# Start of a conditioned attention and MLP block: order of the first loads, modulation, low parts, and the fourth pair's loads

## The chip, the core and the metric

The kernel runs on one core of a Trainium2 chip. The time is that of one execution on the device, in microseconds (us); the median of three runs of the kernel before is shown below, with one further run under the profiler. The engines are TensorE (PE; its weight loads are shown as PEld), VectorE (DVE), ScalarE (ACT), GpSimd (POOL) and SyncE (SP), which issues nearly all transfers.

## The reference

The input x has 2048 tokens of 512 values, c is one row of 512. All is float32.

```
mod = silu(c) @ w_mod                  # six rows of 512: sa, ca, ga, sb, cb, gb
h = layernorm(x) * (1 + ca) + sa
q, k, v = split(h @ wqkv)              # 32 heads of 16
x = x + ga * (softmax(q k^T / 4) v @ wo)
h = layernorm(x) * (1 + cb) + sb
out = x + gb * (mish(h @ w1 + b1) @ w2)   # 1792 in the middle
```

## The kernel before

Each float32 factor of a projection is held as a high part that is rounded to TensorE's fp32r format and a low part, the rest (names in `_h`, `h` and `_l`, `l`: `h_h` and `h_l`, `wh` and `wl`, `qh` and `ql`). A product is three matmuls: high times high, high times low, low times high. `hi_copy(eng, ...)` makes a high part on the engine that is given ("a" ACT, "p" POOL, "v" DVE), `lo_sub` a low part.

Every engine's order is that of the code: the kernel is written under a manual schedule. A small planner (`pe_queue`, `pe_run`, `unit`, hooks at numbered steps) hands out PE's matmuls among the other work; `free_banks` decides from the names of what a piece reads and writes which pieces depend on one another.

The program has four parts.

1. The start (to about 50 us), which holds nearly all of the change. SP loads c (as `cc`, 128 x 4), the two modulation weights that come first (`wma`, sa and ca, 1 MB each), tokens (`xt`, tiles of 128 tokens) and slices of wqkv (`wr`). `first_norm` takes the statistics of tokens 0 to 511 on DVE (BN_STATS, BN_AGGR) and the scales on POOL; `first_apply` normalises a tile; `sil` is silu(c); `modc` has the modulation as columns, `modc[:, 0]` sa and `modc[:, 1]` 1 + ca. Both come from eight 32x512 matmuls (one for each 128 rows of the weight, in 32 partitions each), a copy to `row`, and sixteen matmuls with the 0/1 column `sel`, which add the four parts and turn the row into a column. Then a loop over blocks of 512 tokens (`tb` = 0 to 3): `tr_tb` transposes the normalised tiles on PE into PSUM, makes `h_h` on ACT, the full value `hf` on DVE and `h_l` = `hf` − `h_h` on DVE for the quarters k in `LOV[tb]`, else on POOL; `qk_unit` and `v_unit` project; `stats_tb` and `apply_tb` normalise the blocks that follow. `slice_split` makes `wh` and `wl` of a slice of wqkv.
2. The maxima (to about 102 us): the first two head pairs' scores are made once and DVE takes the maxima of their rows (L555). They are put into the query tiles by four loads from `mt` to `qa` (L577). Projections fill PE.
3. The main loop of steps t: for each pair of heads scores (L588), exponentials on ACT (L591), values (L606), and the scores and maxima of a pair to come (L539, L541). `load_pair(pp)` loads queries (`qa`, L313) and keys (`ka`, L322) of a pair from scratch memory at a hook; the step of the hook counts in half steps of t, negative before the main loop.
4. The tail of the MLP.

`qa` and `ka` hold constant rows (zeros, ones) which are set once at the start; `zer` is a tile of zeros. POOL sets all of them before it does anything else.

Of the kernel before, what the change touches and what calls it, by code (L numbers as in the profile page):

```python
# [18 lines left out]
def adaln_block(ctx: ExitStack, tc: tile.TileContext, x, wqkv, wo, w1, b1, w2, c, w_mod, out):  # L19
    nc = tc.nc  # L20
    P = 128
# [27 lines left out]
    out = out[0]  # L49

    ctx.enter_context(tc.manual_schedule())
    nc.scalar.preload_act_table_set("natural_log_exp_and_others")
# [19 lines left out]
    nc.gpsimd.memset(hcap, HCAP)  # L72
    ones = cst.tile([P, 1], F32, name="ones")
    nc.gpsimd.memset(ones, 1.0)
    sel = cst.tile([P, 1], F32, name="sel")
    nc.gpsimd.memset(sel, 0.0)
    for k in range(DK):
        nc.gpsimd.memset(sel[32 * k:32 * k + 1, :], 1.0)
    lows = cst.tile([P, 1], F32, name="lows")
    nc.vector.tensor_reduce(out=lows[:32], in_=ident[:32, :32].rearrange("p (a v q) -> p v a q", a=4, v=2)[:, 1], op=ALU.add,  # L80
                            axis=AX.XY)
# [18 lines left out]
    def lo_sub(eng, lo, src, hi):  # L100
        (nc.gpsimd if eng == "p" else nc.vector).tensor_sub(lo, src, hi.bitcast(F32))  # L101
# [66 lines left out]
    def free_banks():  # L168


        seen = []
        for i in nc.cur_bb.bb.instructions:
            banks, names, made = set(), set(), set()
            for a in (*i.outs, *i.ins):
                v = getattr(a, "bass_ap", None)
                if v is not None and v.tensor.name != ring_t.tensor.name:
                    names.add(v.tensor.name)
                    if any(a is w for w in i.outs):
                        made.add(v.tensor.name)
# [148 lines left out]

    with ExitStack() as es:
        lp = es.enter_context(tc.tile_pool(name="lp", bufs=1))  # L330
        cc = lp.tile([P, DK], F32, name="cc")
        nc.sync.dma_start(cc, c.rearrange("o (k p) -> p (o k)", p=P))
        xts = []

        def load_x(t):
            xt = lp.tile([P, D], F32, tag="xt", name="xt", bufs=16)
            nc.sync.dma_start(xt, x[t * P:(t + 1) * P, :])
            xts.append(xt)

        wma = [lp.tile([P, DK, D], F32, name=f"wma{i}") for i in range(2)]  # L340
        for i in range(2):
            nc.sync.dma_start(wma[i], w_mod[:, i * D:(i + 1) * D].rearrange("(k p) m -> p k m", p=P))
        for t in range(4):
            load_x(t)
        slice_load(1, 0, lp, lp)
        slice_load(0, 0, lp, lp)
        for t in range(4, 8):
            load_x(t)
# [2 lines left out]
            load_x(t)  # L351
        slice_load(0, 1, pw)
        zer = lp.tile([P, TB], F32, name="zer")
        nc.gpsimd.memset(zer, 0.0)
        for i in range(NR):
            nc.gpsimd.memset(qa[i].bitcast(F32), 0.0)
        for i in range(2):
            nc.gpsimd.memset(ka[i].bitcast(F32), 1.0)

        e = lp.tile([P, DK], F32, name="sil_e")  # L360
        nc.scalar.activation(e, cc, AF.Exp, scale=-1.0)
        nc.vector.tensor_scalar_add(e, e, 1.0)
        nc.vector.reciprocal(e, e)
        nc.vector.tensor_mul(sil, cc, e)

        rss = {}

# [19 lines left out]
        def first_norm():  # L387

            mv = lp.tile([P, 4, 2], F32, tag="ln_mv4", name="ln_mv4", bufs=2)
            rs = lp.tile([P, 4, 4], F32, tag="ln_rs4", name="ln_rs4", bufs=3)  # L390
            for h in range(2):
                two = slice(2 * h, 2 * h + 2)
                for i in range(2 * h, 2 * h + 2):
                    st_ = lp.tile([P, 6], F32, tag="ln_st", name="ln_st", bufs=4)
                    nc.vector.bn_stats(out=st_, in_=xts[i])
                    nc.vector.bn_aggr(out=mv[:, i, :], in_=st_)
                nc.gpsimd.tensor_scalar(rs[:, 0, two], mv[:, two, 1], 1.0, EPS, op0=ALU.mult, op1=ALU.add)
                nc.gpsimd.tensor_scalar(rs[:, 3, two], mv[:, two, 0], -1.0, 0.0, op0=ALU.mult, op1=ALU.add)
                nc.gpsimd.tensor_tensor(rs[:, 1, two], rs[:, 0, two], nhalf.to_broadcast([P, 2]), op=ALU.pow)
                nc.gpsimd.tensor_mul(rs[:, 2, two], rs[:, 3, two], rs[:, 1, two])  # L400
                if h == 0:
                    hi_k = split_hi(1, 0)
            return rs, hi_k

        def split_hi(kind, i, eng="p"):
# [4 lines left out]
        def split_lo(kind, i, hi):  # L410
            lo = lp.tile([P, DK, P], F32R, tag="wl", name="wl", bufs=2)
            lo_sub("p", lo, slices[kind, i], hi)
            slices[kind, i] = (hi, lo)

        def first_apply(rs, i, eng):
            xt = xts[i]
            if eng == "a":
                nc.scalar.activation(xt, xt, AF.Identity, scale=rs[:, 1, i:i + 1], bias=rs[:, 2, i:i + 1])
            else:
                nc.vector.tensor_scalar(xt, xt, rs[:, 1, i:i + 1], rs[:, 2, i:i + 1], op0=ALU.mult, op1=ALU.add)  # L420

        def first_tr():
            pts = [bank(("ring", "ms", "ring", "acc")[k]) for k in range(DK)]
            for ii in ((0,), (1,), (2, 3)):
                for k in range(DK):
                    for i in ii:
                        nc.tensor.transpose(pts[k][:, i * P:(i + 1) * P], xts[i][:, k * P:(k + 1) * P], ident)
            return pts

        def tr_tb(tb, ks=range(DK), pts=None):  # L430
            for k in ks:
                if pts is None:
                    pt = bank(("ring", "ms", "ring", "acc")[k])
                    for i in range(4):
                        nc.tensor.transpose(pt[:, i * P:(i + 1) * P], xts[4 * tb + i][:, k * P:(k + 1) * P], ident)
# [4 lines left out]
                nc.scalar.activation(h_h[:, k, s], pt, AF.Identity, scale=modc[:, 1, k:k + 1], bias=modc[:, 0, k:k + 1])  # L440
                nc.vector.tensor_scalar(hf, pt, modc[:, 1, k:k + 1], modc[:, 0, k:k + 1], op0=ALU.mult, op1=ALU.add)
                lo_sub("v" if k in LOV[tb] else "p", h_l[:, k, s], hf, h_h[:, k, s])

        rs, hi_k = first_norm()
        pr, pm = [], bank()[:, :2 * DK].rearrange("p (i k) -> p i k", k=DK)
        for i in range(2):
            pr.append(ring())
            for k in range(DK):
                nc.tensor.matmul(pr[i][32 * k:32 * k + 32, :], sil[:, k:k + 1].to_broadcast([P, 32]), wma[i][:, k, :],
                                 start=True, stop=True)  # L450
        for i in range(2):
            row = lp.tile([P, D], F32, tag="hf", name="row", bufs=6)
            nc.scalar.copy(row, pr[i])
            for k in range(DK):
                nc.tensor.matmul(pm[:, i, k:k + 1], row[:, k * P:(k + 1) * P], sel, start=True, stop=True)
        for i in range(2):
            first_apply(rs, i, "a")
        split_lo(1, 0, hi_k)
        hi_q = split_hi(0, 0, "a")
        split_lo(0, 0, hi_q)  # L460
        first_apply(rs, 2, "a")
        first_apply(rs, 3, "v")
        nc.vector.tensor_scalar_add(modc[:, 1, :], pm[:, 1, :], 1.0)
        nc.vector.tensor_copy(modc[:, 0, :], pm[:, 0, :])
        stats_tb(1)
        tr_tb(0, pts=first_tr())
        apply_tb(1)
# [11 lines left out]
        for tb in range(NB):  # L479
            if tb + 2 < NB:  # L480
                stats_tb(tb + 2)
            if tb == 0:
                slice_split(2, 0, eng="v")
            parts = []
            early = []
            for kind in (1, 0) if tb == 0 else (1,):
# [1063 lines left out]
```

## Time and profile before

| what | value |
| --- | --- |
| median of 3 runs | 1690.82 us (1689.89 to 1692.33) |
| profiled execution | 1691.02 us, of it 1689.2 us span |
| PE busy | 1667.3 us, 99% of the span |
| DVE, ACT, POOL busy | 1441.5, 1355.1, 821.1 us |
| chain that ended last | PE 91%, DVE 3%, ACT 3%, DMA 2%, POOL 1% |

The busy share is a mean over the span. The start differs from the rest: PE begins at 9.21 us. In the timeline, each row has the start, the length, the engine, the line of the kernel, the operation, and what is written and read; a bracket at its end tells how long the engine had stood idle before and whose work released it. In rows of groups, the numbers behind the first bar are the busy time in us and the mean of one in ns.

### The profile page before, as it was taken

What the parts mean: (1) busy time and instruction counts of PE and PEld (TensorE: products, weight loads), DVE (VectorE), ACT (ScalarE), POOL (GpSimd) and SP (SyncE); (2) the same over time, 40 slices, a digit from 0 to 9 for tenths busy, and PEclk for the clock granted to TensorE, in tenths of its full rate; (3) what the DMA queues carried; (4) which work ended last, traced back from release to release, by engine and by line L of the source; (5) the groups of instructions that cost most, each with busy time, mean ns of one, the idle gap of its engine ahead of it and who ended that gap; (6) DMA issues with size and microseconds to landing.
All of it is one profiled execution on the core that took longest, in us unless ns stands there. A gap on an engine that the chain in (4) does not pass through costs nothing.

```text
span 1689.2 us, 33772 instructions
## 1 busy us (share of the span) xinstructions
PE 1667.3 (99%) x12418; PEld 921.5 (55%) x12418; DVE 1441.5 (85%) x2369; ACT 1355.1 (80%) x2612; POOL 821.1 (49%) x843
## 2 busy tenths in 40 slices
PE   7999999999999999999999999999999999999999
PEld 5755655555444455555555455555555455555687
DVE  8898888888989988888889888888889888883377
ACT  6257777777778998888888998888888998889674
POOL 7555224655313564556323564556323565555442
PEclk9999999999999999999999999999999999999999
DMA  7877556777755443434355434534354533533261
GB/s 248 269 244 199 147 150 185 218 223 216 231 142 146 110 94 98 117 88 129 84 137 152 115 77 93 139 77 127 87 144 122 130 94 77 144 107 132 75 230 63
DMA packets 115406, 238.98 MB, mean 141 GB/s; under 512 B 24928, under 2 KB 50544, under 8 KB 109288
## 3 DMA queue, kind: packets, MB, share of 16 engines
q1 hardware_dynamic: 115240, 236.82, 49.9%
q8 instruction: 98, 1.61, 0.4%
q14 instruction: 68, 0.56, 0.1%
HBM read 180.48 MB, written 51.45 MB: 137 GB/s over the span
## 4 chain that ended last, share of the span: by engine, by line
PE 91%; DVE 3%; ACT 3%; DMA 2%; POOL 1%; issue 1%; SPq 0%; ACTq 0%; DVEq 0%; POOLq 0%
PE bk L606 29%; PE ring L588 22%; PE ring L539 20%; PE bk L139 11%; PE bk L132 3%; PE ring L1219 2%; PE ring L132 2%; DVE mx L541 2%; ACT pr L591 1%; PE ring L553 0%; DMA qa<-mt 0%; DMA xt<-in_A_x 0%; PE ring L922 0%; DMA kscr<-qh 0%; PE ring L568 0%
## 5 line engine op out<-in xcount | busy, mean ns | idle before, releaser
L541 DVE TENSOR_REDUCE mx<-ring 128x1 f32<-128x512 f32 x1968 | 1223.1, 682 | 150.0 <-PE ring L539 136.4
L591 ACT ACTIVATE pr<-ring 128x512 f32<-128x512 f32 x2048 | 1078.4, 603 | 207.1 <-PE bk L139 124.7
L539 PE MATMUL ring<-ka,qa 64*128 64x512 f32 x1968 | 817.9, 429 | 1.4 <-ACT pr L591 1.1
L588 PE MATMUL ring<-qa,ka 64*128 64x512 f32 x2048 | 759.1, 402 | 3.4 <-ACT pr L591 1.9
L606 PE MATMUL bk<-pr,vg 128*32 128x512 f32 x4096 | 545.1, 604 | 0.0
L539 PEld LDWEIGHTS ring<-ka,qa 64*128 64x128 f32 x1968 | 350.5, 184 | 326.2 <-DVE mx L541 251.3
L588 PEld LDWEIGHTS ring<-qa,ka 64*128 64x128 f32 x2048 | 373.7, 184 | 194.7 <-DVE mx L541 111.4
L139 PE MATMUL bk<-h,w 64*128 64x512 f32 (+1 forms) x1080 | 278.1, 390 | 0.0
L139 PE MATMUL bk<-w,a_h 64*128 64x512 f32 x632 | 210.9, 413 | 0.0
L139 PEld LDWEIGHTS bk<-h,w 64*128 64x128 f32 x1080 | 178.5, 184 | 9.3 <-ACT pr L591 1.5
L606 PEld LDWEIGHTS bk<-pr,vg 128*32 128x32 f32 x4096 | 81.2, 108 | 135.4 <-issue 126.0
L139 PE MATMUL bk<-w,a_l 64*128 64x512 f32 x316 | 124.0, 392 | 0.0
L139 PEld LDWEIGHTS bk<-w,a_h 64*128 64x128 f32 x632 | 106.8, 184 | 4.3 <-ACT hb L800 1.0
L978 POOL TENSOR_TENSOR y<-yd,y 128x512 f32<-128x512 f32 x44 | 56.9, 1293 | 89.0 <-ACT yd L977 79.7
L812 POOL TENSOR_SCALAR qq<-ee 128x512 f32<-128x512 f32 x25 | 15.5, 619 | 169.6 <-ACT ee L806 169.6
L828 POOL TENSOR_TENSOR qq<-qq,rr 128x512 f32<-128x512 f32 x42 | 54.1, 1289 | 85.9 <-ACT rr L822 85.9
L814 POOL TENSOR_TENSOR hb<-hb,ee 128x512 f32<-128x512 f32 x42 | 54.1, 1288 | 79.6 <-DVE ee L810 77.7
L139 PE MATMUL bk<-w,o_hl 64*128 64x512 f32 x288 | 79.1, 405 | 0.0
L101 POOL TENSOR_TENSOR a_l<-hb,a_h 128x512 fp32r<-128x512 f32 x53 | 73.1, 1379 | 4.4
L98 POOL TENSOR_SCALAR qh<-qf 128x512 fp32r<-128x512 f32 x27 | 16.7, 619 | 90.8 <-ACT qf L262 69.4
L139 PEld LDWEIGHTS bk<-w,a_l 64*128 64x128 f32 x316 | 58.3, 185 | 3.4
L139 PE MATMUL bk<-h_h,wl 64*128 64x512 f32 x168 | 57.2, 420 | 0.2 <-ACT pr L591 0.2
(219 smaller groups left out, 1909.1 us busy)
## 6 DMA issues: line engine op xcount, KB each, us to landing
ka<-kscr SPq DMA_DIRECT2D x124, 384.0 KB
w<-w2scr SPq DMA_DIRECT2D x56, 512.0 KB
w<-w1scr SPq DMA_DIRECT2D x46, 512.0 KB
vg<-vscr SPq DMA_DIRECT2D x32, 552.0 KB
qa<-qscr SPq DMA_DIRECT2D x124, 100.0 KB
kscr<-qh SPq DMA_DIRECT2D x16, 512.0 KB
qscr<-qh SPq DMA_DIRECT2D x32, 256.0 KB
w2scr<-hl SPq DMA_DIRECT2D x14, 512.0 KB
```

The costliest lines, as they stand in the source:

```text
L101: (nc.gpsimd if eng == "p" else nc.vector).tensor_sub(lo, src, hi.bitcast(F32))
L132: nc.tensor.matmul(acc, l, r, start=start, stop=stop)
L139: i = nc.tensor.matmul(acc, l[64 * g:64 * g + 64], r[64 * g:64 * g + 64], start=start and not then, stop=bool(stop and then))
L539: nc.tensor.matmul(pm, qt[64 * s:64 * s + 64, qs * P:(qs + 1) * P], kt[64 * s:64 * s + 64, kb * TB:(kb + 1) * TB], start=True, stop=True)
L541: nc.vector.tensor_reduce(out=mxs[n][:, s, 4 * j + qs, kb:kb + 1], in_=pm, op=ALU.max, axis=AX.X)
L588: nc.tensor.matmul(p_, kt[64 * s:64 * s + 64, kc * P:(kc + 1) * P], qt[64 * s:64 * s + 64, :], start=True, stop=True)
L591: e = nc.scalar.activation(pr, p_, AF.Exp, scale=SCALE)
L606: nc.tensor.matmul(accs[n][32 * h:32 * h + 32, :], vgs[n][:, o:o + 32], pts.pop((t, h)), start=(kc == 0), stop=(kc == 15))
L814: (nc.vector if tail else nc.gpsimd).tensor_mul(hb, hb, ee)
L828: nc.gpsimd.tensor_mul(qq, qq, rr)
L978: nc.gpsimd.tensor_add(y[i], yd, y[i])
L1219: nc.tensor.matmul(po[i // 2][:, i % 2, :], l[:, s], w[:, r, :], start=(f == 0 and j == 0), stop=(f == FT - 1 and j == 2))
```

## The change

- **Loads.** The four tiles of the first tokens come first, then sa's weights, k's slice of wqkv, ca's weights and q's slice. Each modulation weight comes as four loads of 128 rows.
- **c.** It is loaded as four rows (`crow`, issued by ACT ahead of its table load) and turned by a PE transpose. `keep_busy(n)` adds n transposes of the identity into the same PSUM bank, whose results nobody uses: 8 before c's transpose, 30 behind it, 4 ahead of the first projection.
- **Modulation.** The sums are 32 matmuls of 32x128 that accumulate over the weight's rows, so that each output quarter fills 32 partitions; sixteen for sa stand among the first block's transposes, sixteen for ca behind them. DVE copies a 128x128 piece to `row`, PE transposes it, and DVE reads the column out of every 32nd entry. `sel` goes.
- **Engines.** Statistics and scales of the first eight tiles come in pairs (`stats_two`). Tile 3 is normalised on POOL, was on DVE. The ones of `ka[0]` and `ka[1]` are casts on ACT, were memsets on POOL; two `qa` memsets and `zer` come behind tile 3. For k, `wh` is on ACT and `wl` on DVE (both were on POOL); for q both are on POOL.
- **Low parts.** DVE makes `hf` = PSUM × scale − `h_h` in one instruction, and the shift is added behind it: on DVE by a `tensor_scalar` for k in `LOV[tb]`, else on POOL. `LOV[0]` is (2, 3), was (1,).
- **`slice_split(2, 0)`** (v's slice) comes ahead of the statistics of block 2, was behind them.
- **`free_banks`** tells the four 512-token parts of `h_h` apart.
- **The fourth pair** is loaded at hook −4, was −8.

```diff
-    LOV = ((1,), (), (1, 3), (1, 3))
+    LOV = ((2, 3), (), (1, 3), (1, 3))
...
-                    names.add(v.tensor.name)
+                    part = v.offset % (DK * S) // TB if v.tensor.name == h_h.tensor.name else 0
+                    names.add((v.tensor.name, part))
...
-        cc = lp.tile([P, DK], F32, name="cc")
-        nc.sync.dma_start(cc, c.rearrange("o (k p) -> p (o k)", p=P))
+        crow = lp.tile([DK, P], F32, name="crow")
+        nc.scalar.dma_start(crow, c.rearrange("o (k p) -> (o k) p", p=P))
...
+        def load_mod(i):
+            for k in range(DK):
+                nc.sync.dma_start(wma[i][k], w_mod[k * P:(k + 1) * P, i * D:(i + 1) * D])
         for t in range(4):
             load_x(t)
+        load_mod(0)
         slice_load(1, 0, lp, lp)
+        load_mod(1)
         slice_load(0, 0, lp, lp)
...
-        for i in range(NR):
-            nc.gpsimd.memset(qa[i].bitcast(F32), 0.0)
-        for i in range(2):
-            nc.gpsimd.memset(ka[i].bitcast(F32), 1.0)
+        for t in qa[:3]:
+            nc.gpsimd.memset(t.bitcast(F32), 0.0)
+        spare = ring()
+        def keep_busy(n):
+            for _ in range(n):
+                nc.tensor.transpose(spare[:, :P], ident, ident)
+        keep_busy(8)
+        cc = spare[:, P:P + DK]
+        nc.tensor.transpose(cc, crow, ident[:DK, :DK])
+        keep_busy(30)
...
+        hi_copy("a", ka[0], ones.to_broadcast([P, S]))
...
+        def mod_sums(i, ks):
+            for k in ks:
+                for m in range(DK):
+                    nc.tensor.matmul(prs[i][32 * m:32 * m + 32, :P], sil[:, k:k + 1].to_broadcast([P, 32]),
+                                     wma[i][k][:, m * P:(m + 1) * P], start=(k == 0), stop=(k == DK - 1))
+        def mod_cols(i):
+            row = lp.tile([P, P], F32, name=f"row{i}")
+            nc.vector.tensor_copy(row, prs[i][:, :P])
+            nc.tensor.transpose(prs[i][:, P:2 * P], row, ident)
+            cols = prs[i][:, P:2 * P:32]
...
-                nc.vector.tensor_scalar(hf, pt, modc[:, 1, k:k + 1], modc[:, 0, k:k + 1], op0=ALU.mult, op1=ALU.add)
-                lo_sub("v" if k in LOV[tb] else "p", h_l[:, k, s], hf, h_h[:, k, s])
+                nc.vector.scalar_tensor_tensor(hf, pt, modc[:, 1, k:k + 1], h_h[:, k, s].bitcast(F32), op0=ALU.mult,
+                                               op1=ALU.subtract)
+                if k in LOV[tb]:
+                    nc.vector.tensor_scalar_add(h_l[:, k, s], hf, modc[:, 0, k:k + 1])
+                else:
+                    nc.gpsimd.tensor_add(h_l[:, k, s], hf, modc[:, 0, k:k + 1].to_broadcast([P, TB]))
...
+        for q in range(2):
+            stats_two(q)
+        first_apply(3, "p")
+        for t in (*(t.bitcast(F32) for t in qa[3:]), zer):
+            nc.gpsimd.memset(t, 0.0)
+        mod_sums(0, (0, 1))
+        first_apply(0)
+        first_tr(0)
+        mod_sums(0, (2,))
+        first_apply(1)
+        first_tr(1)
+        mod_sums(0, (3,))
+        first_apply(2)
+        first_tr(2)
+        first_tr(3)
+        mod_cols(0)
+        hi_k = split_hi(1, 0, "a")
+        hi_copy("a", ka[1], ones.to_broadcast([P, S]))
+        split_lo(1, 0, hi_k, "v")
+        mod_sums(1, range(DK))
+        mod_cols(1)
+        keep_busy(4)
+        hi_q = split_hi(0, 0, "p")
+        split_lo(0, 0, hi_q, "p")
+        for q in range(2, 4):
+            stats_two(q)
+        tr_tb(0, pts=pts)
...
-    for pp, h in ((2, -22), (3, -8)):
+    for pp, h in ((2, -22), (3, -4)):
```

What stands on DVE between silu(c) and the statistics of the second block, before (`ln_mv4` are the statistics, `bk_213` the modulation's columns in PSUM):

```order
L364 TENSOR_TENSOR sil_96<-cc_129,sil_e_184 128x4
L395 BN_STATS ln_st_191<-xt_135 128x6
L396 BN_AGGR ln_mv4_189<-ln_st_191 128x2
...
L396 BN_AGGR ln_mv4_189<-ln_st_206 128x2
L420 TENSOR_SCALAR xt_141<-xt_141,ln_rs4_190 128x512
L463 TENSOR_SCALAR modc_95<-bk_213 128x4
L464 COPY modc_95<-bk_213 128x4
L374 BN_STATS ln_st_248<-xt_147 128x6
```

And after:

```order
L373 TENSOR_TENSOR sil_89<-ring_94,sil_e_224 128x4
L403 BN_STATS ln_st_234<-xt_133 128x6
L404 BN_AGGR ln_mv2_232<-ln_st_234 128x2
...
L404 BN_AGGR ln_mv2_244<-ln_st_249 128x2
L443 COPY row0_295<-ring_94 128x128
L449 COPY modc_88<-ring_94 128x4
L96 TENSOR_TENSOR wl_302<-wr_145,wh_299 128x512
L443 COPY row1_320<-ring_94 128x128
L447 TENSOR_SCALAR modc_88<-ring_94 128x4
L403 BN_STATS ln_st_334<-xt_153 128x6
```

The normalisation of tile 3 has left DVE, and k's `wl` and the two row copies stand ahead of the second block's statistics.

PE's first rows after, where before it began with the eight 32x512 sums:

```order
L363 MATMUL ring<-ident 128x128
L363 MATMUL ring<-ident 128x128 x7
L367 MATMUL ring<-ident,crow 128x4
L363 MATMUL ring<-ident 128x128 x30
L438 MATMUL ring<-wma_125,sil 32x128
L438 MATMUL ring<-wma_125,sil 32x128 x3
```

The warm-up transposes (L363) stand ahead of all that needs `sil`, and c's own transpose (L367) between them.

SP around the loads of the maxima (`mt`), before; `ka_631` and `qa_110` are the fourth pair's tiles:

```order
L276 DMA kscr<-qh 128x2x512
L277 DMA kscr<-ql 128x512
L313 DMA qa_110<-qscr 50x512 x2
L322 DMA ka_631<-kscr 48x2048 x2
L276 DMA kscr<-qh 128x2x512
L277 DMA kscr<-ql 128x512
L577 DMA qa_107<-mt 2x4x128
```

And after, where the fourth pair's are `qa_103` and `ka_705`:

```order
L272 DMA kscr<-qh 128x2x512
L273 DMA kscr<-ql 128x512
L607 DMA qa_100<-mt 2x4x128
L607 DMA qa_101<-mt 2x4x128
L607 DMA qa_100<-mt 2x4x128
L607 DMA qa_101<-mt 2x4x128
L309 DMA qa_103<-qscr 50x512 x2
L318 DMA ka_705<-kscr 48x2048 x2
L230 DMA wr<-in_A_wqkv 128x4x128
```

The fourth pair's loads have moved behind the key writes and the four rows of maxima.

More of the change, by code (lines that the diff above doesn't have):

```diff
@@ L385, in apply_tb, with stats_two, split_hi @@
                 nc.scalar.activation(xt, xt, AF.Identity, scale=rs[:, 1, i:i + 1], bias=rs[:, 2, i:i + 1])
[L387 to L405, printed above, removed]
+        def stats_two(q):
+            mv = lp.tile([P, 2, 2], F32, tag="ln_mv2", name="ln_mv2", bufs=2)
+            rs = lp.tile([P, 4, 2], F32, tag="ln_rs2", name="ln_rs2", bufs=4)
+            for i in range(2):
+                st_ = lp.tile([P, 6], F32, tag="ln_st", name="ln_st", bufs=4)
+                nc.vector.bn_stats(out=st_, in_=xts[2 * q + i])
+                nc.vector.bn_aggr(out=mv[:, i, :], in_=st_)
+                rss["x", 2 * q + i] = rs[:, :, i:i + 1]
+            nc.gpsimd.tensor_scalar(rs[:, 0, :], mv[:, :, 1], 1.0, EPS, op0=ALU.mult, op1=ALU.add)
+            nc.gpsimd.tensor_scalar(rs[:, 3, :], mv[:, :, 0], -1.0, 0.0, op0=ALU.mult, op1=ALU.add)
+            nc.gpsimd.tensor_tensor(rs[:, 1, :], rs[:, 0, :], nhalf.to_broadcast([P, 2]), op=ALU.pow)
+            nc.gpsimd.tensor_mul(rs[:, 2, :], rs[:, 3, :], rs[:, 1, :])
+        def split_hi(kind, i, eng):
             hi = lp.tile([P, DK, P], F32R, tag="wh", name="wh", bufs=2)
@@ L408, in split_hi, with split_lo, first_apply, first_tr @@
             return hi
-        def split_lo(kind, i, hi):
+        def split_lo(kind, i, hi, eng):
             lo = lp.tile([P, DK, P], F32R, tag="wl", name="wl", bufs=2)
-            lo_sub("p", lo, slices[kind, i], hi)
+            lo_sub(eng, lo, slices[kind, i], hi)
             slices[kind, i] = (hi, lo)
-        def first_apply(rs, i, eng):
-            xt = xts[i]
+        def first_apply(i, eng="a"):
+            xt, rs = xts[i], rss.pop(("x", i))
             if eng == "a":
-                nc.scalar.activation(xt, xt, AF.Identity, scale=rs[:, 1, i:i + 1], bias=rs[:, 2, i:i + 1])
+                nc.scalar.activation(xt, xt, AF.Identity, scale=rs[:, 1, :], bias=rs[:, 2, :])
             else:
[L420 to L428, printed above, removed]
+                nc.gpsimd.tensor_scalar(xt, xt, rs[:, 1, :], rs[:, 2, :], op0=ALU.mult, op1=ALU.add)
+        pts = [bank(("ring", "ms", "ring", "acc")[k]) for k in range(DK)]
+        prs = [ring() for _ in range(2)]
+        def first_tr(i):
+            for k in range(DK):
+                nc.tensor.transpose(pts[k][:, i * P:(i + 1) * P], xts[i][:, k * P:(k + 1) * P], ident)
+        def mod_sums(i, ks):
[8 more added lines that the diff above has]
+            cols = prs[i][:, P:2 * P:32]
+            if i:
+                nc.vector.tensor_scalar_add(modc[:, i, :], cols, 1.0)
+            else:
+                nc.vector.tensor_copy(modc[:, i, :], cols)
         def tr_tb(tb, ks=range(DK), pts=None):
@@ L451, in adaln_block @@
[L451 to L462, printed above, removed]
@@ L468, in constants @@
+        split_lo(1, 0, hi_k, "v")
[7 more added lines that the diff above has]
+        tr_tb(0, pts=pts)
+        for i in range(4, 8):
+            first_apply(i)
+            if i == 5:
+                slice_split(2, 0, eng="v")
         def constants():
```

28 lines of the change are left out of this document (4 added, 24 removed).

## The prediction

> **What bounds the kernel now.** I read the page first, then the table by stretch, the chain of waits and the timeline of the start.
>
> ```profile
> span 1689.2 us, 33772 instructions
> PE 1667.3 (99%) x12418; PEld 921.5 (55%) x12418; DVE 1441.5 (85%) x2369; ACT 1355.1 (80%) x2612; POOL 821.1 (49%) x843
> ...
> 10.00:20.00 10.00, 9.79 (x49) 7.09 (x41) 7.70 (x20) 4.74 (x8) 5.73 (x11) 1.00 1.07 393
> 50.00:60.00 10.00, 10.00 (x70) 7.92 (x71) 8.89 (x9) 2.60 (x6) 6.53 (x4) 1.00 0.59 204
> 90.00:100.00 10.00, 9.88 (x45) 5.96 (x44) 9.29 (x12) 1.55 (x4) 4.75 (x5) 1.00 0.88 270
> 100.00:110.00 10.00, 9.38 (x61) 5.47 (x59) 9.60 (x14) 7.20 (x14) 5.75 (x6) 1.00 1.03 339
> ```
>
> In a stretch the first pair after its length is PE's busy time and count, then PEld, DVE, ACT, POOL, clock, DMA share, GB/s. PE works 1667.3 of 1689.2 us, and from 50 us on it has no gap but 0.12 + 0.62 = 0.74 us around 100 us. The edits reach that PE-bound part only through the moment at which the start hands over. So the time moves one for one with that moment, plus what the moved loads do inside those 0.74 us. The profiled run is 1689.2 in span and 1691.02 in all, 0.2 above the median of 1690.82; I add the shift to the median.
>
> The start, from the timeline (start, length, engine, line; the last bracket is the idle time before and its releaser):
>
> ```profile
> 1.32 0.16 DVE L80 TENSOR_REDUCE lows<-ident 32x1 f32<-32x16 f32 x1 [1.32 <-POOL ident masks.py:199]
> 3.17 0.20 ACT L361 ACTIVATE sil_e<-cc 128x4 f32<-128x4 f32 x1 [1.18 <-DMA cc<-in_c]
> 3.41 5.33 DVE L362 TENSOR_SCALAR sil_e<-sil_e 128x4 f32<-128x4 f32 x1 [1.76 <-ACT sil_e L361]
> 5.16 3.56 POOL L358 MEMSET ka<- 128x2048 f32 x2
> 8.99 0.16 DVE L364 TENSOR_TENSOR sil<-cc,sil_e 128x4 f32<-128x4 f32 x1
> 9.79 0.69 DVE L395 BATCH_NORM_STATS2 ln_st<-xt 128x6 f32<-128x512 f32 x1 [0.64 <-DMA xt<-in_A_x]
> 10.62 0.66 DVE L395 BATCH_NORM_STATS2 ln_st<-xt 128x6 f32<-128x512 f32 x1
> 11.59 0.19 POOL L397 TENSOR_SCALAR ln_rs<-ln_mv 128x2 f32<-128x2 f32 x1 [2.88 <-DVE ln_mv L396]
> 12.81 0.19 POOL L400 TENSOR_TENSOR ln_rs<-ln_rs 128x2 f32<-128x2 f32 x1
> 13.40 1.52 ACT L418 ACTIVATE xt<-xt,ln_rs 128x512 f32<-128x512 f32 x2
> 15.04 2.68 POOL L101 TENSOR_TENSOR wl<-wr,wh 128x512 fp32r<-128x512 f32 x2
> 15.12 1.48 DVE L420 TENSOR_SCALAR xt<-xt,ln_rs 128x512 f32<-128x512 f32 x1 [2.03 <-POOL ln_rs L400]
> 16.21 0.45 PE L427 MATMUL ring<-ident,xt 128*128 128x128 f32 x1
> 16.52 0.15 DVE L463 TENSOR_SCALAR modc<-bk 128x4 f32<-128x4 f32 x1
> 17.33 0.42 PE L427 MATMUL bk<-ident,xt 128*128 128x128 f32 x1
> 17.54 0.42 PE L427 MATMUL ring<-ident,xt 128*128 128x128 f32 x1
> ...
> 19.07 0.78 ACT L440 ACTIVATE h_h<-ring,modc 128x512 fp32r<-128x512 f32 x1 [2.93 <-PE ring L427]
> 19.88 0.81 DVE L441 TENSOR_SCALAR hf<-ring,modc 128x512 f32<-128x512 f32 x1
> 20.98 0.63 PE L132 MATMUL ring<-h_h,wl 128*128 128x512 f32 x1
> 21.45 0.69 DVE L101 TENSOR_TENSOR h_l<-hf,h_h 128x512 fp32r<-128x512 f32 x1
> 22.15 0.39 PE L132 MATMUL ring<-h_h,wl 128*128 128x512 f32 x1
> 22.16 3.79 POOL L101 TENSOR_TENSOR h_l<-hf,h_h 128x512 fp32r<-128x512 f32 x3
> 25.07 1.04 ACT L94 CAST wh<-wr 128x1024 fp32r<-128x1024 f32 x1
> 25.39 0.60 PE L435 MATMUL bk<-ident,xt 128*128 128x128 f32 x4
> 26.70 1.21 DVE L101 TENSOR_TENSOR wl<-wr,wh 128x1024 fp32r<-128x1024 f32 x1
> 27.82 0.81 DVE L441 TENSOR_SCALAR hf<-ring,modc 128x512 f32<-128x512 f32 x1
> ...
> 45.48 1.16 DVE L101 TENSOR_TENSOR h_l<-hf,h_h 128x512 fp32r<-128x512 f32 x1
> 49.36 1.05 PE L132 MATMUL ring<-h_l,wh 128*128 128x512 f32 x2 [1.03 <-POOL h_l L101]
> ```
>
> Three things stand there. A DVE instruction that should take 0.15 us is held 5.33 us, until POOL's memsets end at 8.72. The first tokens land only behind 2 MB of modulation weights, at 9.79. TensorE starts slow: transposes at 17.33 and 17.54 are 0.21 apart, those at 25.39 about half of that (four end within 0.60; I take 0.11), and a projection matmul falls from 0.63 to 0.39 between 20.98 and 22.15, about 5.8 us after the dense work began at 16.2. The granted clock (the 1.00 of the stretches) does not show this.
>
> **The change, part by part.**
>
> *SiLU.* Eight warm-up transposes start at 1.3 and last to 1.3 + 8 × 0.21 = 3.0. The row of c lands at about 3.1, as cc did. Its transpose follows, then 30 more warm-ups. In the program as built the exponential waits on PE's counter at the last of these 30 and not at c's own transpose (all write one PSUM bank). At the slow pitch the 30 take 6.4 us, at the fast one 3.3. With the 5.8 us that the trace shows, the clock opens at 1.3 + 5.8 = 7.1: 18 slow and 12 fast, 3.9 + 1.3 = 5.2, end at 8.4. The exponential and three small steps take about 1.0, so sil stands at 9.4; before, 8.99 + 0.16 = 9.15. The blocked port and the late tokens are cured, and the warm-up takes their place: **+0.25**.
>
> A rule of the Trainium skill bears on this (page "TensorE: Matmul & The Clock Gate", Part 1): the clock opens after one busy free-running window of about 3.4 us. An estimate by that page is opening at 4.7 to 8.1 us, sil at 8.2 to 9.9; the trace's 5.8 lies inside.
>
> *First block.* Four statistics at a pitch of 0.8 (9.79 to 10.62) run from 9.5 to 12.7 (before: 13.1). A POOL chain takes 12.81 + 0.19 − 11.59 = 1.4, so the last scales are there at 14.1. The third apply (0.76) ends on ACT at 14.9, and the cast of wh for k at 15.5. This wl now stands on DVE (0.6 to 0.7), ahead of the second row copy. POOL is then at its own cast of wh for q and the subtraction, so I let wl end at 17.2 (if it waits for nothing: 16.2). Row copy, transpose and add bring the second modulation column to 18.05; before it was 16.67: **+1.4**. The 16 sums of 32x128 and the two row transposes, which replace eight long and eight short matmuls, are off the path: the weights land by about 10.3 (3.25 MB at 393 GB/s, begun 2 us in). The first h_h comes at 18.3, 0.8 earlier than at 19.07, because the token transposes are done by then. But DVE takes the statistics of the next four tiles only behind the column, 18.2 to 21.4, and its first hf moves from 19.88 to 21.45: **+1.6**. ACT's two casts of ones (by the 1.04 for 1024, about 2.1 each) stand ahead of the first apply and ahead of h_h; both end before their followers are due (10.8 and 17.6), so they cost nothing unless the applies come earlier by 2 us.
>
> *Fused low parts.* The nearest row to a fused operation (by group: count, busy us, mean ns), and behind it SP's and PE's rows for the moved loads:
>
> ```profile
> L810 DVE SCALAR_TENSOR_TENSOR ee<-ee 128x512 f32<-128x512 f32 x31 | 22.4, 723 | 15.0 <-ACT ee L806 15.0
> ...
> 88.84 2.49 SPq L313 DMA_DIRECT2D qa<-qscr  x2
> 92.58 0.38 SPq L276 DMA_DIRECT2D kscr<-qh  x1
> 100.58 0.33 SPq L526 DMA_DIRECT2D vg<-vscr  x1
> 108.95 1.07 PE L606 MATMUL bk<-pr,vg 128*32 128x512 f32 x8
> ```
>
> I take 0.72, what the scaling cost as pitch; nothing gained. Adding the bias is the same 1.27 on POOL (3.79 / 3). On DVE it replaces a subtraction of 0.69 alone and 1.16 beside POOL. L420 is the row for it: held until POOL's first subtraction ends at about 16.35, then finished at 16.60, so about 0.2 of work plus the wait. I take 0.2 (ends: 0.2 and 0.69). The Trainium skill has the mechanism (page "SBUF — State Buffer", Who interferes with whom: the pair of ports shared by DVE and GpSimd is an exclusive lock, and tensor_scalar may take it); L420 agrees with it. Without any wait of this kind I get a sum 1.0 lower.
>
> In block 0 two additions go to DVE instead of one subtraction; then the wl for v (1.2) comes, now ahead of the statistics, same work. With POOL's two additions holding the second bias step, DVE reaches hf of block 1 at 30.2 against 27.82: **+2.4**. Blocks 2 and 3 have four DVE low parts which fall from 1.16 to about 0.8 with the wait for POOL: 4 × 0.38 = **−1.55** back. The handover, where PE now waits 1.03 for a low part at 49.36, comes 2.4 − 1.55 = **0.85 later**. With the clock opening at 4.7 I get −0.2, at 8.2 +1.5; with 0.4 or 0.69 for the addition 0.5 or 1.7 more.
>
> *Keeping h apart by 512 tokens* takes waits from the planner's view; the rows of PE, DVE, ACT and POOL behind the start stand in the old order, so zero.
>
> *The fourth pair.* SP's four loads (88.84 to 92.58 with their issue) go behind the four rows of the maxima. The key writes at 92.58 and the maxima come some 3.7 earlier, but the values' load at 100.58 queues behind that pair; PE needs it at 108.95. PE's whole loss there is 0.74, which is the most it could gain. It would be issued at 104.3 at the latest, which leaves 4.6 us. I take 0; bounds −0.74 and, for a landing 2 us too late, +2.
>
> Sum: 1690.82 + 0.85 = **1691.7**.
>
> **The rivals.** *Slower: the clock closes again.* Between the first eight sums (done at 10) and the first apply (12.8) PE has almost nothing to do, and then short bursts. If it falls back, projections from 18.3 to 22 run at half pace (1.85 lost), and transposes and row turns add 0.85: +2.7, hence 1691.7 + 2.7 = 1694.4. Before, no gap of that length followed dense work, so the trace cannot decide; it is against it that the last warm-ups and eight sums leave under 3 us of quiet. It decides if the token transposes at 13 to 16 come at a pitch of 0.21 again. The Trainium skill (same page, HAM oscillation) says that quiet over about 3.4 us closes the gate; no trace here shows that.
>
> *Faster: the exponential passes the warm-ups.* If it waits for c's transpose alone, sil is at 4.3, statistics run 4.4 to 7.6, and the last weights at 10.3 set the column at 13. hf of block 0 comes at 16.4, the handover 4.0 earlier than now: 1686.8. Against it is the built wait; for it, that the two read different columns of the bank. An early clock together with an unblocked port also lies on this side, at −1 to −2.
>
> *Nothing done.* If PE's 1.03 at 49.36 hides the rest, the shift is 0; this is inside my forecast's own range.
>
> **How the numbers follow.** A measurement of this kernel can tell about 0.2%, 3.4 us: 1687.4 to 1694.2. The forecast has 0.50, with its own range 1689.6 to 1693.7 (bounds above); faster 0.28; the closed clock 0.22. The range takes in both rivals' times with a little for the port: 1686.6 to 1694.8. Faster 0.28, same 0.50, slower 0.22.
>
> **What would show it.** Right: sil near 9.4, the 30 warm-ups end near 8.4 with a pitch that halves on the way, second column near 18, hf of block 1 near 30, biases of about 0.2 that start when POOL's addition ends, PE without gap from about 51. Wrong: sil near 4 or 5; transposes at 13 to 16 at 0.21 pitch; a gap of PE before the first values' product near 109.

## The result, and the profile after

The changed kernel took 1696.81 us (median of 7 runs, 1695.27 to 1699.01) against 1690.84 us (7 runs): a ratio of 1.0034, 95% interval 1.0023 to 1.0046, so slower by 6.0 us. The forecast was 1691.7 us; the measured time lies 2.0 us above the upper end of its range, 1694.8. The profiled run is one of the slower ones: 1698.46 us, span 1696.7, 7.5 longer than the span before. One execution of a later kernel (`e_pair_back`) ran throughout at a granted clock of 0.56 and took 2572 us; it is left out of that kernel's time, which rests on the other five.

The table by stretch of the changed kernel (same columns as before):

```profile
span 1696.7 us, 33929 instructions
...
10.00:20.00 10.00, 6.93 (x65) 4.85 (x65) 3.12 (x10) 4.65 (x6) 6.54 (x14) 0.66 1.07 373
90.00:100.00 10.00, 9.88 (x46) 5.94 (x44) 9.32 (x11) 1.96 (x4) 3.53 (x4) 1.00 0.92 335
100.00:110.00 10.00, 8.67 (x51) 5.48 (x51) 9.20 (x13) 5.32 (x10) 3.45 (x4) 1.00 0.79 174
110.00:120.00 10.00, 6.55 (x41) 2.80 (x37) 4.36 (x8) 4.46 (x9) 6.53 (x6) 0.83 1.06 381
```

Two places are new. From 10 to 20 us the granted clock is 0.66, where it was 1.00. And between 100 and 120 us PE loses 1.33 + 3.45 us, where before it lost 0.62 up to 110 and nothing behind. The timeline of the start shows the first:

```profile
3.44 4.57 PE L363 MATMUL ring<-ident 128*128 128x128 f32 x30
8.74 0.16 DVE L373 TENSOR_TENSOR sil<-ring,sil_e 128x4 f32<-128x4 f32 x1
8.96 0.64 PE L438 MATMUL ring<-wma,sil 128*32 128x128 f32 x16 [0.95 <-DVE sil L373]
12.93 0.48 PE L433 MATMUL ring<-ident,xt 128*128 128x128 f32 x1 [3.33 <-ACT xt L424]
13.20 0.42 PE L433 MATMUL bk<-ident,xt 128*128 128x128 f32 x1
13.41 0.42 PE L433 MATMUL ring<-ident,xt 128*128 128x128 f32 x1
20.66 0.16 DVE L447 TENSOR_SCALAR modc<-ring 128x4 f32<-128x4 f32 x1 [0.42 <-PE ring L444]
24.08 0.72 DVE L462 SCALAR_TENSOR_TENSOR hf<-ring,modc,h_h 128x512 f32<-128x512 f32 x1
32.37 0.72 DVE L462 SCALAR_TENSOR_TENSOR hf<-ring,modc,h_h 128x512 f32<-128x512 f32 x1
33.66 0.68 DVE L96 TENSOR_TENSOR ql<-ring,qh 128x512 fp32r<-128x512 f32 x1
53.40 1.22 DVE L585 TENSOR_REDUCE mx<-ring 128x2 f32<-128x1024 f32 x1
```

The warm-ups end at 8.0, and PE is quiet for 3.33 us behind the first sums. The token transposes then come 0.21 us apart, the slow pitch of the kernel before at 17.33 and 17.54. The second modulation column starts at 20.66 (before 16.52), hf of block 1 at 32.37 (27.82). The same places of the kernel before:

```profile
29.26 0.69 DVE L101 TENSOR_TENSOR ql<-ring,qh 128x512 fp32r<-128x512 f32 x1
51.72 1.22 DVE L555 TENSOR_REDUCE mx<-ring 128x2 f32<-128x1024 f32 x1
```

Later DVE wins back part of its delay: the first maxima, the handover to the PE-bound part, are only 1.68 us late. The first low part of a projection, `ql`, is 4.4 us late. `ql` is one of the tiles that SP writes to scratch memory (`kscr`, `qscr`) and reads back (`ka`, `qa`), all in one queue. SP's rows, before, and PE's second group of values' products:

```profile
29.98 0.34 SPq L277 DMA_DIRECT2D kscr<-ql  x1
58.59 1.99 SPq L322 DMA_DIRECT2D ka<-kscr  x4
77.16 3.71 SPq L1466 DMA_DIRECT2D w1scr<-ep  x4
111.78 1.07 PE L606 MATMUL bk<-pr,vg 128*32 128x512 f32 x8
```

and after; behind the dots stand four rows of the chain of waits, then PE's rows of the first two groups of values' products:

```profile
34.37 0.34 SPq L273 DMA_DIRECT2D kscr<-ql  x1
64.61 1.71 SPq L318 DMA_DIRECT2D ka<-kscr  x4
83.45 3.60 SPq L1496 DMA_DIRECT2D w1scr<-ep  x4
104.83 0.68 SPq L556 DMA_DIRECT2D vg<-vscr  x1
...
77.98 0.37 ACT vq L287
81.03 9.44 DMA vscr<-vq
90.53 6.37 DMA qscr<-ql
104.83 10.06 DMA vg<-vscr
114.93 1.93 PE L636 MATMUL bk<-pr,vg 128*32 128x512 f32 x8 [3.15 <-DMA vg<-vscr]
119.31 1.06 PE L636 MATMUL bk<-pr,vg 128*32 128x512 f32 x8
```

SP's delay of 4.4 us at 34 us has grown to 6 at 64 to 83 us; from 55 to 90 us its longest waits are loads of `ka` that wait for the landing of a write to `kscr` (4.3 + 3.2 us). The chain of waits does not pass through the first `ql`, though. It leads from the handover along PE's rows to 77.9 us, over copies and casts on ACT and POOL to SP, and from there through two writes to scratch memory that took 9.44 and 6.37 us and POOL's work behind them to the values' load.

The values' load is issued 4.25 us later than before (100.58) and takes 10.06 us to land, in a stretch in which the DMA engines are busy nearly all the time (0.92, 0.79 and 1.06). In the kernel before, it was there by 108.95, within 8.4 us. PE waits 3.15 us for it. Behind the wait the clock is lower (0.83 from 110 to 120 us), and the products take 1.93 instead of 1.07 us. The second group of products starts at 119.31, where before it stood at 111.78: 7.53 later, which is the whole of the profiled run's difference. Of that, 1.7 is the handover, 3.15 this wait, about 1.0 longer waits for exponentials (0.58 + 0.51 + 0.24 + 0.30 against 0.40 + 0.22), and the rest, about 1.7, mostly the slow clock: from the first group to the second it takes 4.38 us instead of 2.83.

### The profile page after: what moved, and what is told of

Read it like the earlier page. It is cut to its first block, busy times and chain, and to the rows that moved or that the text cites. A ratio compares the mean times of both kernels' runs of the same rounds, so it can differ in the third digit from the quotient of the medians.

```text
span 1696.7 us, 33929 instructions
## 1 busy us (share of the span) xinstructions
PE 1673.3 (99%) x12495; PEld 927.4 (55%) x12495; DVE 1433.2 (84%) x2372; ACT 1357.9 (80%) x2612; POOL 814.6 (48%) x839
## 4 chain that ended last, share of the span: by engine, by line
PE 91%; DVE 3%; ACT 2%; DMA 2%; POOL 1%; issue 1%; SPq 0%; ACTq 0%; POOLq 0%; DVEq 0%
PE bk L636 29%; PE ring L618 22%; PE ring L569 19%; PE bk L134 11%; PE bk L127 2%; PE ring L1249 2%; PE ring L127 2%; DVE mx L571 2%; ACT pr L621 1%; DMA vg<-vscr 1%; DMA vscr<-vq 1%; DMA qa<-mt 0%; PE ring L952 0%; PE ring L583 0%; PE ring L363 0%
```

## The experiments

Each kernel ran against the kernel before on the same chip; the ratio is that of the two with its 95% interval. The times in the last three columns are those of one profiled run, in us: the first `ql` on DVE, the first maxima, the first values' product on PE.

| kernel | ratio | ql | maxima | product |
| --- | --- | --- | --- | --- |
| before | 1 | 29.3 | 51.7 | 108.95 |
| changed | 1.0034 [1.0023, 1.0046] | 33.7 | 53.4 | 114.93 |
| e_pair_alone | 1.0004 [0.9995, 1.0012] | 29.2 | 51.7 | 109.82 |
| e_before_late | 1.0021 [1.0012, 1.0030] | 32.7 | 54.0 | 114.48 |
| e_pair_back5 | 1.0018 [1.0010, 1.0027] | 32.7 | 53.8 | 112.09 |
| e_low | 1.0048 [1.0035, 1.0061] | 34.0 | 57.2 | 115.46 |
| e_open | 1.0013 [1.0004, 1.0021] | 30.5 | 51.5 | 109.67 |
| e_open_back | 1.0017 [1.0009, 1.0026] | 31.4 | 51.2 | 113.71 |
| e_nowarm | 1.0004 [0.9995, 1.0013] | 28.0 | 49.1 | 109.33 |
| e_stats | 1.0022 [1.0013, 1.0031] | 31.4 | 52.4 | 111.45 |
| e_open_stats | 1.0018 [1.0009, 1.0027] | 31.4 | 52.4 | 110.84 |
| e_vg | 1.0022 [1.0012, 1.0031] | 32.3 | 52.1 | 112.76 |
| e_bank | 1.0009 [1.0000, 1.0018] | 27.8 | 47.5 | 109.35 |
| e_bank_back | 0.9994 [0.9986, 1.0003] | 27.3 | 47.0 | 110.68 |
| e_bank_vg | 0.9999 [0.9991, 1.0008] | 28.3 | 48.0 | 109.35 |
| e_bank_vg8 | 0.9982 [0.9973, 0.9991] | 28.2 | 48.5 | 107.53 |
| e_bank_vg8_back | 1.0012 [1.0004, 1.0021] | 28.0 | 47.7 | 112.91 |
| e_before_vg8 | 1.0015 [1.0006, 1.0024] | 29.0 | 51.5 | 110.15 |

The last three columns vary from one execution to the next. The start of `e_vg`, `e_pair_back5` and `e_pair_back_look` is that of the changed kernel, and their first `ql` stands at 32.3, 32.7 and 33.0, not at 33.7: the slow pitch of the transposes ends at 16.3 to 17.4 us there, and lasts to 18 in the trace above. So 1 us in these columns is not a kernel's own.

**The moved loads of the fourth pair.** In the changed kernel back to where they were:

```diff
-    for pp, h in ((2, -22), (3, -4)):
+    for pp, h in ((2, -22), (3, -8)):
```

> The changed kernel with the fourth pair's loads at hook -8 again; all else stays. If the moved loads are what keeps the values' load from landing in time (theory 1), PE's 3.15 us wait for it and the closed clock behind it go, and what is left is the later handover of the start: 1690.8 + 1.7 = 1692.5 us. If the start's delay of SP's chain is enough by itself (theory 2), PE waits for that load here too and the time stays at 1695 to 1697.

> One look at the changed kernel with the fourth pair's loads at hook -8 again. By its earlier times (1693.8 to 1699.5) the loss is not that of the moved loads; then its trace has PE waiting 2 us or more near 110 to 116, for the values' load or for the maxima's rows. If it has no such wait, the loss lies elsewhere.

> The changed kernel with the fourth pair's loads at hook -8 once more, to see what the moved loads add to a late start. Its one look had no wait for the values' load and 1692.9 us, its earlier times a median of 1697.6. Theory A alone (late start is the loss): 1695 to 1697 us, not to be told from the changed kernel. If the moved loads turn a late start into a wait: 1692.5 to 1694 us.

The first set has a median of 1695.7 us and a ratio of 1.0035 [1.0023, 1.0047]; the single execution took 1692.86 us, and the second set 1694.3 us, 1.0018. In the traces of the last two PE no longer waits for the values, and the products start near 112. By their ratios the two sets differ by 3 us, and their intervals overlap only just; the larger second one gives about half of the loss to the moved loads, the first none of it, and neither brings the kernel back to before. The other way round, the kernel before with the loads at −4:

> The kernel before with the fourth pair's loads at hook -4 and nothing else. Theory 1: the values' load is issued some 3.7 us later, PE waits 1 to 4 us for it near 109, 1692 to 1695 us. Theory 2: the start is early here, so the load still lands in time: 1690.8 us, no wait.

Nothing in the time; PE waits 0.90 us for the values besides 0.38 and 0.22 for exponentials. The values' load is issued at 100.67, as before, but takes 9.11 us to land. So the moved loads alone cost nothing that can be measured; at most they turn a late start into a wait.

**Lateness alone.** Six statistics whose results nobody reads, in the kernel before:

```diff
         constants()
+        for i in range(6):
+            st_ = lp.tile([P, 6], F32, tag="ln_st", name="ln_st", bufs=4)
+            nc.vector.bn_stats(out=st_, in_=xts[i])
```

> The kernel before with six more statistics of tiles on DVE (their results unused, about 4.2 us) behind the first four hf: the first ql of DVE comes at 33.4 us instead of 29.3, as in the changed kernel, with nothing else changed. Theory A (a late first ql delays the chain of writes and loads on SP, and the values' load with it): the first values' product begins 3 to 6 us later and the time is 1693.5 to 1697 us. Theory C (PE takes up a late DVE and the change's loss has other causes): the handover moves by 1 to 2 us and the time by no more: 1691.5 to 1693 us.

Theory A holds for the time (1694.8 us, by the interval 2.0 to 5.1 us more than before), but not for its last link. The profiled execution is one of the slower ones, 1697.45 us:

```profile
32.73 0.68 DVE L101 TENSOR_TENSOR ql<-ring,qh 128x512 fp32r<-128x512 f32 x1
105.60 0.62 POOL L98 TENSOR_SCALAR qh<-qf 128x512 fp32r<-128x512 f32 x1 [4.92 <-DMA kscr<-qh]
106.14 0.34 SPq L529 DMA_DIRECT2D vg<-vscr  x1
107.61 0.59 ACT L262 COPY qf<-bk 128x512 f32<-128x512 f32 x1 [4.89 <-POOL ql L101]
108.75 0.50 PE L542 MATMUL ring<-ka,qa 64*128 64x512 f32 x1 [1.72 <-ACT pr L594]
114.48 1.06 PE L609 MATMUL bk<-pr,vg 128*32 128x512 f32 x8
```

The values are not waited for here. POOL waits 4.92 us for a write of keys, ACT 4.89 us with a copy for POOL, and PE for the exponentials behind that copy. Here the late start is paid for through another transfer around 100 us than in the changed kernel. The edit makes all of DVE's work behind it late, the handover too, by 2.3 us; it does not tell a late `ql` from a late handover.

**The closed clock.** Thirty more transposes in the quiet of 3.3 us, once with the pair as changed and once back:

```diff
         mod_sums(0, (0, 1))
+        keep_busy(30)
```

> The changed kernel with 30 more transposes of the identity behind the first eight modulation sums, so that PE is not quiet from 9.6 to 12.9 us. If quiet closes the clock, the first token transposes now come 0.11 us apart, not 0.21, the second modulation column about 2 us earlier (18.7, not 20.7), the first ql of DVE before 32, and the handover 1.5 to 2.5 us earlier; with theory 2 the wait for the values goes and the time is 1690 to 1692 us, with theory 1 most of the wait stays: 1694 to 1695 us. If the clock closes for another reason, nothing changes: 1696.8 us.

> Both: 30 more transposes behind the first sums, and the fourth pair's loads at hook -8. By either theory the wait for the values is gone; the start is by my working 0 to 0.9 us later than in the kernel before: 1690.5 to 1691.7 us.

The quiet was what closed the clock:

```profile
12.76 0.27 PE L433 MATMUL bk<-ident,xt 128*128 128x128 f32 x1
12.87 0.27 PE L433 MATMUL ring<-ident,xt 128*128 128x128 f32 x1
```

The transposes come 0.11 apart, the second column at 17.5, and 1.0034 falls to 1.0013: some 3.6 us of the loss of 6.0. DVE's first `ql` is still 1.2 us later than before. With the pair moved back there is no further gain (1.0017). PE then waits for the rows of the maxima, which come behind the pair in SP's queue:

```profile
102.73 0.46 PE L619 MATMUL ring<-qa,ka 64*128 64x512 f32 x1 [1.45 <-DMA qa<-mt]
```

**The warm-ups and SiLU.** First without the 30 warm-ups, then with c's transpose in another PSUM bank, so that SiLU does not wait for them (the lines that allocate that bank move up with it):

```diff
-        cc = spare[:, P:P + DK]
+        cc = prs[1][:, 2 * P:2 * P + DK]
```

> The changed kernel without the 30 warm-up transposes behind c's own. If silu(c) waits only for the warm-ups, it stands at about 4.4 us instead of 8.9, the first statistics end near 8, and the first token transposes (slow as in the changed kernel) begin near 9; the whole start is bound by the weights' landing (10.3 us) and by DVE, and the first ql of DVE comes at 29 to 31, not 33.7: 1691 to 1693 us. Rival: without the warm-ups the clock stays slow through the sums and the first projections, which costs what the early start brings: 1695 to 1698 us.

> The changed kernel with c's transpose in another PSUM bank than the 30 warm-ups, which stay. The exponential then waits for c's transpose alone: silu(c) at 4.4 us, statistics at 5 to 8, and the sums follow the warm-ups at 8 with no quiet of 3 us in front of the first apply, so the clock stays fast. If lateness of the start is the whole loss, the first ql stands at 27 to 29 us and the time is 1687 to 1690.5 us. Rival: DVE's order (weights' low part, second column and statistics one behind the other) is what is late; then the gain stays under 2 us: 1695 us.

SiLU stands at 4.24 and 4.17 us: it did wait for the warm-ups. Taking them out gives back nearly the whole loss (1.0004). With the other bank the warm-ups stay and the maxima begin 4.2 us earlier than in the kernel before (1.5 earlier than without warm-ups), and the time is still not shorter. So no run shows a gain in time from the warm-ups. The rows of the kernel with the other bank; the three at 79.39, 86.48 and 99.80 are from its chain of waits:

```profile
52.00:102.00 50.00, 48.03 (x272) 33.39 (x272) 45.66 (x45) 10.53 (x23) 25.37 (x26) 1.00 0.82 256
...
47.52 1.22 DVE L585 TENSOR_REDUCE mx<-ring 128x2 f32<-128x1024 f32 x1
59.56 1.71 SPq L318 DMA_DIRECT2D ka<-kscr  x4
79.39 7.03 DMA w1scr<-ep
86.48 8.10 DMA kscr<-qh
99.80 9.51 DMA vg<-vscr
100.59 0.49 PE L569 MATMUL ring<-ka,qa 64*128 64x512 f32 x1 [1.41 <-ACT pr L621]
109.35 1.91 PE L636 MATMUL bk<-pr,vg 128*32 128x512 f32 x8 [1.89 <-DMA vg<-vscr]
```

PE gives the 4.2 us up again before the first values' product: it comes at 109.35, where it came at 108.95. Its waits are for an exponential and for the values' load, and the chain behind them has three transfers of 7 to 9.5 us each, with POOL's work between the last two. In SP's queue the early start is gone long before: the first `ql` is 1.5 us earlier than in the kernel before, but the load of `ka` at 59.56 is 1.0 later than its counterpart there (58.59).

**DVE's order.** The statistics of tiles 4 to 7, and POOL's two steps for q's slice ahead of them, moved in front of `mod_sums(0, (0, 1))`, alone and with the 30 transposes:

> The changed kernel with the statistics of tiles 4 to 7 (and POOL's two steps for q's slice) ahead of the modulation columns, into DVE's idle 12.1 to 16.3 us. The clock stays closed from 13 to 18 as in the changed kernel. If DVE's order is the loss, the first hf comes right behind the second column, near 21 instead of 24.1, the first ql near 30.5, and the time is 1691 to 1693 us. If the closed clock is the loss, 1695 to 1697 us.

> Both: 30 more transposes behind the first eight sums and the statistics of tiles 4 to 7 early. First hf near 18, first ql 27.5 to 28.5, no wait of PE for the values' load: 1688 to 1690 us, less than the kernel before. If what is lost there lies behind the start (the moved loads), it stays at 1692 to 1693 us.

The first hf comes at 21.43 instead of 24.08, and the ratio is 1.0022 against 1.0034; the intervals overlap, so a gain is not shown. With the clock open it adds nothing: both kernels have the second column at 20.42, and in the second PE waits 1.57 us for a row copy on DVE behind these statistics.

**The low parts.** The old form in the changed kernel, with `LOV[0] = (1,)`:

> The changed kernel with the old low parts (scale and shift in one instruction, then a subtraction; for the first block quarter 1 on DVE): tells what fusing them brings. By the traces DVE's fused step takes 0.72 to 0.75 as the old one's pitch, its shift 0.25 plus the wait for POOL, POOL's addition 1.04 alone against 1.28: so the old form is 0 to 1.5 us slower from the start's end on: 1696.8 to 1698.3 us. If the fused form is a loss in this start, 1694 to 1696 us.

1.0048 against 1.0034: the fused form looks like a gain of 2.4 us here, though the intervals still overlap. The maxima begin 3.84 us later than in the changed kernel (57.24), but the first values' product only 0.53 later.

**The values' load.** At hook −4 (behind the rows of the maxima) or −8:

```diff
-    at(-3, lambda: load_v(0))
+    at(-4, lambda: load_v(0))
```

> The changed kernel with the first values' load right behind the four rows of maxima (hook -4, was -3), ahead of the fourth pair and of two key writes; nothing else. If this load's landing sets the end (theory A), it lands some 3 us earlier, PE's wait of 3.15 us and the slow clock behind it go: 1691.5 to 1693 us. If the transfers of that stretch as a whole are what is late (theory B), the wait only moves to another load (the maxima's rows, the fourth pair): 1695 to 1697 us.

The changed kernel gains less than theory A says: 1695.0 us. The wait moves, as theory B has it:

```profile
110.87 0.62 ACT L89 CAST wh<-wr 128x512 fp32r<-128x512 f32 x1 [2.67 <-DMA wr<-in_A_wqkv]
112.04 0.79 PE L569 MATMUL ring<-ka,qa 64*128 64x512 f32 x1 [2.60 <-ACT pr L621]
112.76 1.93 PE L636 MATMUL bk<-pr,vg 128*32 128x512 f32 x8
```

ACT waits for a slice of wqkv that is also queued behind the fourth pair, and holds the exponentials with it. With the early SiLU:

> The early SiLU (c's transpose in a bank of its own) and the values' load behind the maxima's rows. With the early SiLU alone the maxima began 4.2 us earlier than in the kernel before, and PE lost all of it again by waiting for that load. Theory A: 1688 to 1690 us, faster than the kernel before. Theory B: 1691.5 to 1693 us as with the early SiLU alone.

> The same with the values' load still earlier, at hook -8, ahead of two key writes and of the maxima's rows. Theory A: as the last or better by the rest of the wait, 1687.5 to 1690 us. Theory B: the maxima's rows come later for it, and PE waits for them: 1692 to 1694 us.

> The early SiLU with the fourth pair's loads at hook -8 again and the values' load at -3. In the late start, hook -8 for the pair brought about half of the loss back. If the loads' order around the maxima is what takes the early start's gain, the wait for the values' load goes here too: 1688 to 1690 us. If the early values' load is needed for it, 1691 to 1693 us, as the early SiLU alone.

> The early SiLU with both the values' load and the fourth pair's loads at hook -8, in this order, ahead of two key writes and the maxima's rows. In the kernel before the early values' load cost 0.15%, so the rows of maxima, now behind 1.5 MB, should come late: 1690 to 1693 us, slower than with the pair at hook -4 (1687.9). If the transfers fit into the time that the early start leaves, 1687 to 1689 us.

> The kernel before with the first values' load at hook -8 and nothing else. It waits for that load hardly at all (0.25 us), so the earlier load brings nothing by itself: 1690.8 us within 0.1%. If the gain of the best kernel so far comes from this alone, 1688 to 1689 us.

Only the early SiLU together with the values at −8 and the pair at −4 is faster than the kernel before: 1687.9 us, 0.9982 [0.9973, 0.9991]. In its trace the product starts at 107.53, 1.4 earlier than before; but the profiled execution is the slowest of its 11, 1692.47 us, and waits 2.2 us for rows of maxima between 300 and 400 us (before 1.2), so the trace does not show the faster executions. The same early load in the kernel before costs 0.15%. With the values at −3 and the pair at −8 the early SiLU brings nothing (0.9994), and with both at −8 the gain is gone (1.0012). In these two PE waits for the rows of the maxima, in this order:

```profile
99.89 0.76 PE L618 MATMUL ring<-qa,ka 64*128 64x512 f32 x1 [2.71 <-DMA qa<-mt]
102.58 0.76 PE L618 MATMUL ring<-qa,ka 64*128 64x512 f32 x1 [4.72 <-DMA qa<-mt]
```

So with the early start the pair at −8 holds up the maxima's rows, and the pair at −4 the values' load (1.89 us in `e_bank`). With the pair at −4 and the values at −4 or −8 PE waits for neither before the first product; what it still loses there to exponentials is 3.30 us with −4 and 2.52 with −8. Why only the latter is faster is not shown, since the one trace of it is of its slowest execution.

## Why the prediction was wrong

- **SiLU behind the warm-ups: right.** Forecast 9.4, in the trace 8.74 + 0.16 = 8.90, because the clock opened sooner: the 30 took 4.57 us, not 5.2. In the other full-clock traces in which SiLU waits for them they took 4.24 to 5.39 us, and SiLU was done at 8.57 to 9.72. A bank of its own brought SiLU to 4.2.
- **The clock closing again: the rival that I gave 0.22.** I counted the quiet as under 3 us; it was 3.33. Its sign was shown by the transposes 0.21 apart, its share by `e_open`, about 3.6 us of the 6.0. The rival's time, 1694.4, was still 2.4 short. Its price was taken mostly as slow projections, but by 22 us the clock was open again (a projection took 0.39 at 22.26); what it cost was the second column, done at 20.82 instead of 18.05. The Trainium skill (page "TensorE: Matmul & The Clock Gate", Part 1, HAM oscillation) has quiet beyond about 3.4 us closing the gate. The 3.33 us of quiet here, behind 0.64 us of small sums, is close to that figure and just short of it, so the trace does not confirm it as a limit.
- **DVE's order: right in direction, short in size.** hf of block 1 moved by 4.55 us, not 2.4, of which 2.8 is the later column. The fused step took 0.72 to 0.74 (I took 0.72). The shift on DVE waits for POOL as L420 did: the one that starts at 48.18 and takes 0.70 ended 0.29 behind POOL's addition. That addition took 1.04 alone, where I had 1.27. DVE won back 2.9 us by the handover, not 1.55 (and 4 × 0.38, my sum for it, is 1.52). So the handover came 1.68 late, against my 0.85.
- **"The time moves one for one with that moment": this step failed.** `e_bank` hands over 4.2 us earlier than the kernel before and `e_nowarm` 2.7 earlier, and neither is faster (1.0009 and 1.0004). The edits reach the PE-bound part also through the transfers. In the changed kernel PE lost 4.78 us between 100 and 120 us, where it had lost 0.62. What stands on the chain of waits there is, in the changed kernel and in `e_bank`, writes to scratch memory of 6.37 to 9.44 us each and then the values' load, 10.06 and 9.51 us. The time is settled only behind them: from the start of the second group of values' products to the end of the span, 18 of the 19 profiled executions at full clock take 1576.3 to 1579.1 us, and the other, of `e_bank_vg8`, 1580.3; from the handover to the end they take 1637.1 to 1644.7. I had read 0.74 us of lost PE time as a sign of slack (and only up to 140 us: by the traces PE also loses 5.8 us from 300 to 1600 us before, and 5.1 after). The chain of waits of the kernel before has this row, which I did not use:

```profile
92.58 7.33 DMA kscr<-qh
```

  A write of keys was on the chain for 7.33 us: the transfers were on the point of being late already.
- **The fourth pair: taken as 0, at worst +2.** I left the values' load 4.6 us to land. It took 10.06 and held PE for 3.15 us. By itself the move costs nothing (1.0004). The victim that I named, the values' load, is right; the slice of wqkv behind the same loads, for which ACT holds the exponentials, I did not list.
- **The fast rival** (SiLU free of the warm-ups, 1686.8) had the handover right, −4.2 by trace and −4.0 forecast, but partly by luck: the first hf came at 18.17, not at 16.4, and DVE won back more behind it. Its time was wrong by the same failed step, 1692.75.

What is open: how much the moved loads add in the late start (the two sets differ by 3 us), whether the statistics' place matters there, how a late start turns into just this loss (`e_before_late` loses 3.4 us in the median for a handover 2.3 later, which one for one would still allow), and what the other parts of the change do singly: the order of the loads, the sums, tile 3 on POOL and the casts on ACT were not taken back one by one.

## What to carry to other kernels

A start that ends in a PE-bound stretch can still set the time through the transfers that it feeds: follow the chain of waits from the handover on to the last load that PE needs, and compare issue and landing times there, not only the engine's handover. Warm-up work is to be checked for what waits behind it: here SiLU waited for all 30 warm-ups, the quiet of 3.33 us that followed undid them, and the kernel without them lost nothing that could be measured. Before a load is moved, list everything that is queued behind its new place, those for ACT's casts too, and everything behind its old one.

## What the runs showed of the hardware

The granted clock and the pitch of transposes do not go together: before, transposes 0.21 apart stood in a stretch with 1.00; after, the same pitch stood at 0.66. How long a wait has to be to slow PE is not shown: behind waits of 1.84 us (`e_nowarm`) and 1.85 us (`e_stats`) for the values' load the products took 1.07 us, behind 1.89 us (`e_bank`) 1.91. POOL's addition with a broadcast second operand took 1.04 us where a subtraction with two full operands took 1.28.
